# Depthwise causal convolution and token-mixing MLP on one core: the turn of y moves from TensorE to VectorE, the query matmul to 32-row tiles, with new chunks, banks, ring and order

## The chip, the cores and the metric

The kernel runs on one core of a Trainium2 chip. The metric is the device time of one execution in microseconds (us). Three runs of the kernel before took 170.6, 169.86 and 170.9 us; their median is 170.6 us.

## The reference, cut to what matters

```python
w = softmax(weight)                      # 8 heads x 7 taps
y[b, s, h, :] = sum_k w[h, k] * x[b, s - 6 + k, h, :]     # zeros ahead of token 0, 24 channels a head
wq, wk = y @ w_q, y @ w_k                # 192 -> 64
W_tok  = einsum('bsd,btd->bst', wq, wk) / sqrt(64)
mixed  = einsum('bst,btd->bsd', W_tok, y)
out    = relu(mixed) @ w_out             # 192 -> 192
```

`x` is 8 batches x 4224 tokens x 192 channels in float32, 25.95 MB, and `out` has the same size. Both kernels use that the token mix is linear: `mixed = wq @ (w_k^T (y^T y)) / 8`. So for each batch they need the 192x192 matrix `y^T y` (the "gram"), a 64x192 matrix M made from it, and then `relu(wq @ M) @ w_out`, token by token.

## The kernel before, in words

Work goes batch by batch; while batch b is convolved, turned and multiplied, batch b-1 is mixed and stored.

- **Load** (`gen_load`, L483; the DMA is issued at L513 by GpSimd). A batch is cut into 35 chunks of 122 tokens. A chunk lies on 128 partitions: 6 tokens of history and 122 of its own. The DMA turns float32 into bfloat16. `XW` holds all eight batches, so no load waits for a buffer.
- **Convolution** (`gen_conv`, L585). For each pair of heads TensorE multiplies the chunks by a 128x128 band matrix (`BAND`), whole (L315) or as two halves of 64 columns (L316, L317). ScalarE or VectorE moves the result from PSUM to `Y` in bfloat16 (L621): tokens on the partitions, 192 channels in the free dimension.
- **Turn** (`gen_transpose`, L627, and `gen_transpose_hi`, L662). The query matmul needs channels on the partitions. TensorE transposes the first 128 channels of each chunk (L321 whole, or L322 and L323 in halves) and the last 64 channels (L678; two chunks at a time, side by side). VectorE copies these out of PSUM to `YTL` (L648) and `YTH` (L688).
- **Queries** (`gen_wq`, L693). For each of five blocks of tokens TensorE multiplies `w_q` with `YTL` (128 rows, L707) and `YTH` (L711), two column tiles of 64 side by side, 512 tokens in each; a copy brings the result to `WQT` (L728).
- **Gram** (`gen_gram`, L732): three matmuls of 64 columns for each chunk (L744), in a PSUM bank of its own, bank 7. **Mix weights** (`gen_mix_weights`, L758): M from the gram.
- **Mix** (`gen_mix`, L821): M times queries (L836, and L848 or L856), ReLU out of PSUM (L873 on ScalarE, L874 on VectorE), times `w_out` (L902, L920), copy to `OUT` (L941), store from SP (L949).

The order of all this is written out by hand in `PLAN`: a list of turns, each with an operation's number, a letter for its engine or its form on TensorE, and its PSUM bank. Every engine executes its own operations in this order and never passes one that waits. `Program.place` puts in the semaphore waits that the data and the banks ask for.

Of the kernel before, what the change touches and what calls it, by code (L numbers as in the profile page):

```python
# [10 lines left out]
F32 = mybir.dt.float32  # L11


PLAN = """
1D 38G 2D 13G 37G 39G 40G 8D 19D 41G 42G 9D 56G 57G 14D 58G 59G 60G 61G 62G 63G 5D 64G 15P 65G 12D 66G 67G
68G 69G 70G 71G 72G 73G 74G 0S 22D 75G 20D 76G 77G 78G 23D 24D 25A 16P6 6D 79G 80G 21D 11D 81G 26D 27D 17P
4D 28D 18A 29D 30P5 7D 33P6 34D 35D 31A 32A 36P 84F4 85D 90F3 91A 88P1 89D 86P5 87A 116P5 142P 94P2 95D 92F1
93A 96F3 43S 98F6 99A 97D 118F4 117D 106F5 102F1 104F3 82G 100F6 143P 107D 144P 3D 105A 103A 101D 145P 83G
110F5 108F6 109A 112F3 113A 111D 119D 114F0 120F1 115A 126P2 127D 130P6 131D 47A 124F0 48A 125D 46A 44S
122F5 128P2 146P 10D 147P 121D 49A 140P4 53A 50A 132P0 123D 138P3 129D 134P2 141D 148A 149P6 52A 133A 159P4  # L20
157P0 150D 45S 51A 151F6 135A 139D 160A 155F2 158D 161F4 154A 153A 152A 222P6 136P0 162A 137A 211P1 156D
171P4 197P 54A 224A 167P2 168A 213D 165P5 172D 169P0 198P 170A 166D 221P3 210P5 163P0 199P 55A 173F2 223D
225P3 212A 217P5 164A 214P0 226P 174D 179F2 218F 180D 219D 215F 227A 177F2 178D 244F4 175F3 216A 220S 181P5
264P0 233P6 202P 176D 243P2 246A 265A 182D 228P4 232P0 245A 235D 229P 254P6 256A 201P 234A 262P2 230D 231S
185P6 186D 263A 268P4 266P0 267A 200P 255P6 269D 195P3 187P2 196A 203D 239P4 236P0 257D 258P6 240F 188A 241A
183P3 184D 204F2 205A 237F 259F 247P4 250P2 248F 251F 238A 242S 260D 261S 249A 270F0 271A 189P6 190A 304P
276P4 277A 274P0 206P6 252D 253S 272P2 305P 191P4 208A 207A 209A 328P5 275D 273A 317P0 192D 330A 288P2 289D
290P3 278P4 279D 193P5 194D 318F6 329F2 319A 286F0 340F1 280F4 320A 321P5 331A 291D 332P2 287D 342A 335P0
322P 323A 281D 333P 336P 337A 309P 292P4 284F5 334D 338S 324P2 339P0 361P6 363A 325F 293D 282F4 341A 351P6
285D 298P5 353A 326D 327S 373P0 371P2 283D 306P 374A 302P4 303A 294P6 295A 375P0 299D 372D 300P5 301D 369P2  # L30
296P4 297D 362P6 307P 376A 343P0 350P4 370A 346P2 344P 364A 385F6 347F 352A 345D 308P 310D 357P0 348A 349S
365P4 354P2 358P 386D 311F5 312D 355F 356D 359A 360S 387F6 388D 313F5 316A 315A 366F 377F0 383F2 314A 447P5
411P 425P6 378A 384D 379P0 380D 367A 368S 449A 381P3 427A 436P2 438D 412P 424P5 435P0 382A 397P3 395P4 398D
389F2 426A 428P5 396D 431P3 437A 429P 432P 458P0 390D 430A 414P 460A 457P1 459A 442P5 433D 434S 439P3 415P
440F 441A 443F 444D 445S 446P1 468P0 413P 476P3 482P5 470A 448A 399P0 393P1 416P 469P2 483A 417A 477D 400D
478F3 453P5 471A 479A 394D 450P0 418F2 419D 454F 455A 451F 480F3 391F2 409P5 452A 456S 481D 401P6 402A 464P0
461P3 465P 466A 472P6 462P 392D 403P2 410D 463D 467S 492P5 493D 488P0 489A 518P 490P3 404D 407P5 491A 484P0
# [22 lines left out]
913P 924P0 914A 915S 920P2 925P 926A 927S 941F6 943D 921F 932P4 953P0 955D 952P6 933P 922A 923S 940P2 942A  # L60
936P0 954D 937P 956P6 957P 934D 935S 944P2 945F 948P4 949P 938A 939S 958D 959S 946A 947S 950A 951S
""".split()

COL2, ROW2, FULL = "128x64", "64x128", "128x128"


class Op:


    n = 0  # L70
# [134 lines left out]
def bass_lightweight_conv__then__hypermixer_token_mlp_kernel(  # L205
# [11 lines left out]
    GRP = D // H  # L217
# [814 lines left out]
```

## Time and profile before

| | |
|---|---|
| runs | 170.6, 169.86, 170.9 us; median 170.6 us |
| profiled execution | span 168.6 us from the first to the last instruction; the median run is 2.0 us longer than this span |
| instructions in it | 6398 |
| granted TensorE clock, mean | 0.994 |
| DMA packets | 48154, 40.31 MB as written, mean 239 GB/s |
| POOL | 30.3 us busy, nearly all of it issuing the loads |

How to read the lines below: the page's first part gives each engine's busy time and its share of the span. PE is TensorE's matmuls and PEld its weight loads, DVE is VectorE, ACT is ScalarE, POOL is GpSimd, SP the engine that issues the stores. The timeline lists instructions by start in us, then the time to the end of the last one in the row, then the form `out<-in` with partitions x columns, then the count. TensorE's matmuls overlap, so the duration of one (some 0.2 to 0.4 us) is much more than what it costs in a stream: that is read from the distance between starts. The windows view gives busy time by engine in a stretch, the granted clock, the mean busy share of the 16 DMA engines (over 1 where packets overlap) and the bytes written by DMA per second.

### The profile page before, as it was taken

Reading aid. Unit: us, or ns where it says so; the run is one execution under the profiler, and the core shown is the slowest. Engines: PE = TensorE matmul, PEld = TensorE weight load, DVE = VectorE, ACT = ScalarE, POOL = GpSimd, SP = SyncE. Lnnn points to the kernel's source line nnn. Section 1 sums busy time; section 2 is a strip of 40 time slices with the busy share of each in tenths; the row PEclk is TensorE's granted clock in tenths of the full one; section 3 lists DMA queues with packets and bytes.
Section 4 is the critical chain, followed back from the end, with each engine's and each line's share of the span. In section 5 each row is a group of like instructions: output and inputs, shape, how many; then the busy total and the mean of one; then the engine's idle time right before and its main releaser. Section 6 shows DMA issues by size and latency. Waiting matters only on the chain.

```text
span 168.6 us, 6398 instructions
## 1 busy us (share of the span) xinstructions
PE 158.3 (94%) x2874; PEld 116.1 (69%) x2882; DVE 116.2 (69%) x201; ACT 123.8 (73%) x207; POOL 30.3 (18%) x39
## 2 busy tenths in 40 slices
PE   6978999999999999999999999999999999999980
PEld 1458846876677886777865867787778777884640
DVE  5745878774678777566999686875957758578640
ACT  3233699798977869888566978578897889568970
POOL 7999553530503120000000000000000000000000
PEclk9999999999999999999999999999999999999997
DMA  2999999999999999999999999996644463095897
GB/s 23 172 190 185 205 191 196 189 241 301 263 328 208 300 268 276 299 251 317 284 287 199 289 282 341 235 273 232 231 176 190 189 257 149 0 368 218 315 363 283
DMA packets 48154, 40.31 MB, mean 239 GB/s; under 512 B 37632, under 2 KB 40960, under 8 KB 48128
## 3 DMA queue, kind: packets, MB, share of 16 engines
q0 software_dynamic: 36128, 13.61, 67.6%
q1 hardware_dynamic: 12000, 26.31, 43.1%
q8 instruction: 22, 0.36, 0.8%
q14 instruction: 4, 0.03, 0.1%
HBM read 27.56 MB, written 25.95 MB: 317 GB/s over the span
## 4 chain that ended last, share of the span: by engine, by line
PE 78%; ACT 8%; DMA 4%; DVE 3%; issue 2%; POOL 1%; POOLq 0%; ACTq 0%
PE ps L744 14%; PE ps L902 12%; PE ps L920 9%; PE ps L316 8%; PE ps L321 5%; PE ps L836 5%; DMA out_dram<-out_sb 4%; PE ps L678 4%; PE ps L707 4%; ACT y L621 4%; PE ps L711 3%; PE ps L856 3%; PE ps L315 3%; PE ps L322 3%; PE ps L317 2%
## 5 line engine op out<-in xcount | busy, mean ns | idle before, releaser
L621 ACT CAST y<-ps 122x864 bf16<-122x864 f32 (+3 forms) x48 | 37.2, 794 | 11.6 <-PE ps L315 5.8
L873 ACT ACTIVATE rt<-ps 128x1024 bf16<-128x1024 f32 (+3 forms) x56 | 38.7, 725 | 8.3 <-PE ps L836 6.8
L941 ACT COPY out_sb<-ps 128x768 f32<-128x768 f32 (+1 forms) x43 | 32.6, 779 | 11.9 <-PE ps L920 11.3
L513 POOL DMA_DIRECT2D xw<-in_x_dram x34 | 29.9, 909 | 29.4 <-issue 28.6
L941 DVE COPY out_sb<-ps 128x768 f32<-128x768 f32 (+1 forms) x29 | 23.9, 831 | 14.0 <-PE ps L920 12.7
L744 PEld LDWEIGHTS ps<-y 122*64 122x64 bf16 x840 | 29.4, 110 | 5.3 <-issue 2.2
L744 PE MATMUL ps<-y 122*64 122x64 bf16 (+3 forms) x840 | 32.8, 221 | 0.1
L648 DVE COPY ytl<-ps 128x976 bf16<-128x976 bf16 (+1 forms) x40 | 23.3, 592 | 7.2 <-PE ps L321 4.1
L621 DVE CAST y<-ps 122x816 bf16<-122x816 f32 (+3 forms) x24 | 21.5, 902 | 8.1 <-PE ps L317 5.4
L316 PE MATMUL ps<-xw,band 128*64 128x408 bf16 (+2 forms) x104 | 24.9, 342 | 0.0
L317 PE MATMUL ps<-xw,band 128*64 128x408 bf16 (+2 forms) x104 | 24.9, 342 | 0.0
L920 PE MATMUL ps<-wol,rt 64*128 64x192 bf16 (+1 forms) x264 | 23.9, 248 | 0.4
L902 PE MATMUL ps<-woh,rt 64*128 64x192 bf16 x264 | 22.4, 250 | 0.8 <-ACT out_sb L941 0.3
L874 DVE TENSOR_SCALAR rt<-ps 128x512 bf16<-128x512 f32 (+3 forms) x24 | 18.0, 755 | 3.1 <-PE ps L848 1.4
L920 PEld LDWEIGHTS ps<-wol,rt 64*128 64x128 bf16 (+1 forms) x264 | 15.2, 113 | 5.0 <-PE ps L902 2.5
L902 PEld LDWEIGHTS ps<-woh,rt 64*128 64x128 bf16 x264 | 11.7, 114 | 6.8 <-issue 1.8
L728 DVE CAST wqt<-ps 128x512 bf16<-128x512 f32 (+1 forms) x24 | 14.0, 583 | 2.8 <-PE ps L711 2.5
L688 DVE COPY yth<-ps 128x732 bf16<-128x732 bf16 x24 | 12.5, 534 | 4.5 <-PE ps L678 4.2
L902 PE MATMUL ps<-wol,rt 64*128 64x192 bf16 x177 | 15.4, 243 | 0.0
L711 PE MATMUL ps<-yth,wqh 128*64 128x512 bf16 (+1 forms) x72 | 14.9, 361 | 0.0
L707 PE MATMUL ps<-ytl,wql 128*64 128x512 bf16 (+1 forms) x72 | 14.5, 367 | 0.0
L321 PE MATMUL ps<-ident,y 122*128 122x122 bf16 (+1 forms) x159 | 12.0, 217 | 0.9 <-ACT y L621 0.7
(117 smaller groups left out, 209.8 us busy)
## 6 DMA issues: line engine op xcount, KB each, us to landing
out_dram<-out_sb SPq DMA_DIRECT2D x28, 768.0 KB, 7.3
xw<-in_x_dram POOLq DMA_DIRECT2D x7, 816.0 KB, 40.3
xw<-in_x_dram POOLq DMA_DIRECT2D x7, 768.0 KB, 42.9
out_dram<-out_sb SPq DMA_DIRECT2D x8, 384.0 KB, 3.1
xw<-in_x_dram POOLq DMA_DIRECT2D x2, 432.0 KB, 7.3
out_dram<-out_sb SPq DMA_DIRECT2D x8, 96.0 KB, 5.1
xw<-in_x_dram POOLq DMA_DIRECT2D x1, 384.0 KB, 5.1
xw<-in_x_dram POOLq DMA_DIRECT2D x8, 45.8 KB, 28.0
```

The lines of the kernel that those rows point to most:

```text
L316: e.matmul(out[0:64], lhsT[:, 0:64], rhs, **k)
L317: return e.matmul(out[64:128], lhsT[:, 64:128], rhs, **k)
L321: return e.transpose(out, in_, identity)
L513: lambda e, op, part=part: e.dma_start(*part),
L621: return e.copy(dst, src) if op.engine == "ACT" else e.tensor_copy(dst, src)
L648: lambda e, op: e.tensor_copy(YTL[:, t0:t1], bank(mm_l.bank).bitcast(BF16)[:, 0:cols]),
L707: last = e.matmul(ps[64 * i : 64 * i + DH, 0:n], WQL[:, :], YTL[:, starts[i] : starts[i] + n], start=True, stop=False)
L744: mm = e.matmul(bank(GB)[p : p + 64, o : o + z - r], Y[0:w, yb, c, r : r + 64], Y[0:w, yb, c, r:z], start=st, stop=end, skip_group_check=True,
L873: return e.activation(dst, src(), AF.Relu)
L902: last = e.matmul(bank(op.bank + a)[:, (i - q) * D : (i - q) * D + D], RT[p, slot, a if lo else 2, i:n:nt], WOL[p, :] if lo else WOH[p, :] ...
L920: last = e.matmul(bank(fh.bank + a)[:, (i - q) * D : (i - q) * D + D], RT[p, slot, a, i:n:nt], WOL[p, :], start=False, stop=True, skip_gro ...
L941: return e.copy(dst, src) if op.engine == "ACT" else e.tensor_copy(dst, src)
```

## The change

- **Chunks.** A batch is cut into two halves of 2112 tokens, each into 18 chunks of 120 tokens (the last has 72), so 36 chunks in place of 35. A chunk has 8 tokens of history and 120 of its own on 128 partitions. `BAND` now writes 4 blocks of 32 rows, in each 30 tokens and two rows of zeros.
- **Turn.** `gen_transpose` and `gen_transpose_hi` are gone, with their PSUM banks and copies. In `gen_turn` VectorE transposes `Y` to `YT` in blocks of 32x32, from SBUF to SBUF, with two bfloat16 channels taken as one 32-bit word: four instructions a batch, each 128 partitions x 864 words. After it a block of 32 partitions holds 32 pairs of channels of 30 tokens. There is one `YT`, for one batch.
- **Queries.** `gen_wq` makes two passes of nine chunks in each half. A pass is 48 matmuls of 32 rows (one block) x 64 columns of weights x 270 tokens: 3 groups of channel pairs x even and odd x 4 blocks x 2 halves, so eight tiles of the array are addressed in turn, into four PSUM banks. The moving operand takes every second element. Two copies of 128 x 540 a pass put the result in order in `WQT`. `w_q` is loaded with its rows in pairs and four times, once for each block.
- **Banks.** All eight PSUM banks are dealt out by `PLAN`; the gram has none of its own.
- **Ring.** `XW` has six places; loads of batch 6 and 7 wait until the convolutions of batch 0 and 1 have read theirs.
- **Order.** `PLAN` is new throughout, and with it the share of each engine in the copies. Loads aren't issued strictly by batch any more (the second half of batch 3 and the first of batch 4 go ahead of the first half of batch 3). The three scalings of M (`ms`) and the casts of the weights may now go to VectorE too. The first run-up of TensorE's clock is 4 + 4 + 1 whole matmuls.

On TensorE, around the queries of an early batch (at 47.2 us of the trace), this stood before (`ytl`, `yth` are the turned channels, `ident,y` a transposition, `wqt` a mix):

```order
L707 MATMUL ps<-ytl,wql 64x512 x2
L711 MATMUL ps<-yth,wqh 64x512 x2
L848 MATMUL ps<-wqt,mbd 128x512 x2
L321 MATMUL ps<-ident,y 128x122 x2
L321 MATMUL ps<-ident,y 128x76
L848 MATMUL ps<-wqt,mbd 128x512
L321 MATMUL ps<-ident,y 128x122 x8
```

and this stands at the queries of a middle batch now:

```order
L812 MATMUL ps<-woh,rt 128x192 x8
L829 MATMUL ps<-wol,rt 128x192 x8
L625 MATMUL ps<-yt,wq 64x270 x96
L754 MATMUL ps<-wqt,msb 128x512 x4
L762 MATMUL ps<-wqt,mbd 128x512 x2
L276 MATMUL ps<-xw,band 128x432 x6
```

The queries were five groups of four, strewn among transpositions and mixes; now both passes of a batch mostly stand as one block of 96, and no transposition of `y` is left on this engine.

On VectorE this stood before, in a middle batch:

```order
L728 CAST wqt<-ps 128x512
L688 COPY yth<-ps 128x732
L648 COPY ytl<-ps 128x976
L728 CAST wqt<-ps 128x512
L688 COPY yth<-ps 128x732
L648 COPY ytl<-ps 128x320
L648 COPY ytl<-ps 128x976
L941 COPY out_sb<-ps 128x2x384
```

and this now:

```order
L722 TENSOR_SCALAR msb<-ps 128x128
L722 TENSOR_SCALAR mbd<-ps 64x64
L645 CAST wqt<-ps 128x2x9x30
L606 STREAM_TRANSPOSE yt<-y 128x864 x2
L781 TENSOR_SCALAR rt<-ps 128x1024
L606 STREAM_TRANSPOSE yt<-y 128x864 x2
L645 CAST wqt<-ps 128x2x9x30 x2
L592 CAST y<-ps 128x2x18x24
```

The copies of turned channels, 64 in all, are gone; 32 transpositions stand in their place, and more of the ReLUs of 1024 columns (`rt`) do.

The diff, cut to its core:

```diff
-    XW = sbuf("xw", [128, B, NCC, D], BF16)
-    Y = sbuf("y", [128, 2, NCC, D], BF16)
-    YTL = sbuf("ytl", [128, S], BF16)
-    YTH = sbuf("yth", [128, (NCC - SPLIT // CW) * CW], BF16)
+    XW = sbuf("xw", [128, NX, NC, D], BF16)
+    Y = sbuf("y", [128, 2, NC, D], BF16)
+    YT = sbuf("yt", [128, NYT, NC, D], BF16)
...
-    GB = 7
-    planner = Planner(nbank=7)
+    planner = Planner()
...
+        free = [c for (bb, g), ops in conv_of.items() if bb == b - NX for c in ops]
...
+                    needs=[*free, *part[2]],
...
-    def gen_transpose(b, cs):
-                last = turn_halves(e, ps[:, o : o + w], Y[0:w, yb, c, 0:LO], IDENT[0:w, 0:w], op.mode)
...
-                lambda e, op: e.tensor_copy(YTL[:, t0:t1], bank(mm_l.bank).bitcast(BF16)[:, 0:cols]),
...
+    def gen_turn(b, half, k):
+        yb, tb = b % 2, b % NYT
+        c0 = half * NK + k * PASS
+        def turn(e, op):
+            src = Y[:, yb, c0 : c0 + PASS, :].rearrange("p c d -> p (c d)").bitcast(U32)
+            dst = YT[:, tb, c0 : c0 + PASS, :].rearrange("p c d -> p (c d)").bitcast(U32)
+            return e.transpose(dst, src)
+        needs = [*{r.number: r for c in range(c0, c0 + PASS) for r in y_done[b, c]}.values(), *wq_of.get((b - NYT, k), [])]
...
+    def gen_wq(b, k):
+            for j in range(3):
+                for s in range(2):
+                    for i in range(NBLK):
+                        p = slice(32 * i, 32 * i + 32)
+                        for half in range(2):
+                            c0 = half * NK + k * PASS
+                            last = e.matmul(
+                                bank(op.bank[i // 2] + i % 2)[DH * half : DH * half + DH, 0 : PASS * BLK],
+                                WQ6[p, j, s, :],
+                                YT[p, tb, c0 : c0 + PASS, 64 * j + s : 64 * j + 2 * BLK : 2],
+                                start=j == 0 and s == 0,
+                                stop=j == 2 and s == 1,
+                            )
```

More of the change, by code (lines that the diff above doesn't have):

```diff
@@ L11 @@
 F32 = mybir.dt.float32
+U32 = mybir.dt.uint32
 PLAN = """
[L15 to L19, printed above, removed]
```

831 lines of the change are left out of this document (380 added, 451 removed).

## The prediction

> **What bounds the kernel now.** I read the page's first part, its slices and its chain, then the windows, to see which engine has no slack and whether that changes along the run.
>
> ```profile
> PE 158.3 (94%) x2874; PEld 116.1 (69%) x2882; DVE 116.2 (69%) x201; ACT 123.8 (73%) x207; POOL 30.3 (18%) x39
> DVE  5745878774678777566999686875957758578640
> DMA  2999999999999999999999999996644463095897
> GB/s 23 172 190 185 205 191 196 189 241 301 263 328 208 300 268 276 299 251 317 284 287 199 289 282 341 235 273 232 231 176 190 189 257 149 0 368 218 315 363 283
> PE 78%; ACT 8%; DMA 4%; DVE 3%; issue 2%; POOL 1%; POOLq 0%; ACTq 0%
> ```
>
> TensorE is busy 158.3 of 168.6 us and the chain of waits runs through it for 78% of the span, through the DMA for 4%. So TensorE sets the time from the first chunk to the last stores, and what leaves it is worth its whole price until something else has no slack. The windows say what stands next.
>
> ```profile
> 12.00:25.00 13.00, 12.10 (x212) 8.79 (x210) 10.09 (x20) 8.67 (x23) 9.43 (x12) 1.00 1.55 194
> 60.00:80.00 20.00, 19.98 (x362) 14.85 (x361) 13.52 (x22) 16.49 (x27) 0.12 (x1) 1.00 1.32 280
> 140.00:164.00 24.00, 22.85 (x414) 15.32 (x411) 16.72 (x27) 18.85 (x33) 0.00 (x0) 1.00 0.61 228
> ```
>
> (Columns: stretch, then busy us of PE, PEld, DVE, ACT, POOL, the granted clock, the DMA share, GB/s.) From 60 to 80 us TensorE lacks 0.02 us of 20 at the full clock, with ScalarE at 16.5 and VectorE at 13.5. From 140 us, with ScalarE at 79%, it lacks 1.15 us of 24. In the slices the DMA is busy all the time for 27 of 40, up to 114 us, where the loads end: it is off the chain, but has little to give.
>
> **The change part by part.** *Transpositions and old queries leave TensorE.* Their price in a stream is the distance between starts in the timeline; their counts stand in the groups:
>
> ```profile
> 46.13 0.83 PE L678 MATMUL ps<-ident,y 122*64 122x122 bf16 x24
> 46.80 0.22 PE L322 MATMUL ps<-ident,y 122*64 122x122 bf16 x1
> 47.22 0.39 PE L707 MATMUL ps<-ytl,wql 128*64 128x512 bf16 x2
> 47.44 0.38 PE L711 MATMUL ps<-yth,wqh 128*64 128x512 bf16 x2
> 48.56 0.59 PE L321 MATMUL ps<-ident,y 122*128 122x122 bf16 x8
> 49.09 0.36 PE L902 MATMUL ps<-woh,rt 64*128 64x192 bf16 x4
> ```
>
> ```profile
> L321 PE MATMUL ps<-ident,y 122*128 122x122 bf16 x154 | 11.8, 217 | 0.9 <-ACT y L621 0.7 <-issue 0.2
> L678 PE MATMUL ps<-ident,y 122*64 122x122 bf16 x288 | 11.5, 218 | 0.1
> L322 PE MATMUL ps<-ident,y 122*64 122x122 bf16 x118 | 9.1, 217 | 0.9 <-ACT y L621 0.7
> L711 PE MATMUL ps<-yth,wqh 128*64 128x512 bf16 x64 | 13.3, 379 | 0.0
> ```
>
> The high channels: 24 in 46.80 - 46.13 = 0.67 us, 28 ns each, x288 = 8.0 us. The low channels in halves: eight pairs from 46.80 to 47.22, 53 ns a pair, x118 = 6.2 us; whole: eight from 48.56 to 49.09, 66 ns each, x154 = 10.2 us; the eight short chunks 0.4 us. The queries: a pair of 512 columns takes 47.44 - 47.22 = 0.22 us; 64 such pairs (32 of L707, 32 of L711) are 14.1 us, and the eight short blocks some 0.9 us. In all 39.8 us leave TensorE.
>
> *New queries.* 8 batches x 2 passes x 48 = 768 matmuls of 270 columns on tiles of 32 rows. Nothing in this trace has that form, so I bound it. Below: the pair of 512 columns in 0.22 us is 0.43 ns a column, so 270 columns stream in 116 ns; if all eight tiles work at once, that is 14.5 ns a matmul, 11.1 us in all. Above: only the two column tiles work at once, as they do for L707, and the four row blocks take turns: 116 / 2 = 58 ns, 44.5 us. Between them stands how fast one weight load with its matmul can follow another:
>
> ```profile
> 92.79 0.35 PE L316 MATMUL ps<-xw,band 128*64 128x432 bf16 x1
> 92.81 0.35 PE L317 MATMUL ps<-xw,band 128*64 128x432 bf16 x1
> 96.30 0.19 PE L315 MATMUL ps<-gsb,wkt 128*128 128x64 bf16 x1
> 96.38 0.19 PE L315 MATMUL ps<-gsb,wkb 128*128 128x64 bf16 x1
> 55.10 0.66 PE L744 MATMUL ps<-y 122*64 122x192 bf16 x17
> ```
>
> The second half of a convolution starts 20 ns behind the first, with a weight load of its own between them. The matmuls of 64 columns from 96.30 to 96.38 (three steps) stand 27 ns apart, but that is what 64 columns stream in (64 x 0.43 = 28 ns), so they bound the issue only from above. I take 20 ns, the nearest row for neighbours on different tiles: 768 x 20 = 15.4 us. The range keeps 14.5 and 28 ns (11.1 and 21.5 us); 58 ns is a rival.
>
> The page "TensorEngine Tiling (Array Packing)" of the Trainium skill, section "Instruction Overhead", speaks against small matmuls: about 60 cycles each whatever the free dimension, and it warns against splitting a dimension that is already small. At the 2.4 GHz of "TensorE: Matmul & The Clock Gate" that is an estimated 25 ns, 19.2 us in all, 3.8 us more than my term. The 20 ns above is a little under it, so the trace does not fully agree; no run here shows it for 32 rows.
>
> *One chunk more.* 36 in place of 35: the gram's three matmuls, 18 of which (the 17 of the last row and one behind) stand in the half microsecond from 55.10, cost 0.09 us a chunk; the convolution's 8 heads x 24 columns cost 192 x 0.43 = 0.08 us. x8 = 1.4 us.
>
> *TensorE's sum:* 168.6 - 39.8 + 15.4 + 1.4 = 145.6 us of span, if it stays as dense as now.
>
> *VectorE and ScalarE.* The turn replaces copies out of PSUM:
>
> ```profile
> L648 DVE COPY ytl<-ps 128x976 bf16<-128x976 bf16 x32 | 21.0, 661 | 6.7 <-PE ps L321 3.6 <-PE ps L323 3.0
> L688 DVE COPY yth<-ps 128x732 bf16<-128x732 bf16 x24 | 12.5, 534 | 4.5 <-PE ps L678 4.2
> L648 DVE COPY ytl<-ps 128x320 bf16<-128x320 bf16 x8 | 2.5, 316 | 0.5 <-PE ps L321 0.5
> L621 DVE CAST y<-ps 122x864 bf16<-122x864 f32 x8 | 8.3, 1050 | 1.2 <-PE ps L315 0.8 <-PE ps L317 0.4
> L874 DVE TENSOR_SCALAR rt<-ps 128x1024 bf16<-128x1024 f32 x7 | 8.5, 1217 | 0.2 <-PE ps L836 0.2
> L874 DVE TENSOR_SCALAR rt<-ps 128x512 bf16<-128x512 f32 x12 | 8.2, 684 | 2.0 <-PE ps L848 1.4 <-PE ps L856 0.7
> L728 DVE CAST wqt<-ps 128x512 bf16<-128x512 f32 x18 | 12.3, 685 | 1.9 <-PE ps L711 1.8
> ```
>
> Copies of 36.0 us go (21.0 + 12.5 + 2.5). The 32 transpositions of 864 words have no row. Below: at the rate of the 976-column copy, 864 / 976 x 661 = 585 ns. Above: two cycles a word, twice the 864-column cast, 2100 ns. I take that cast itself, 1050 ns, the row with as many 32-bit columns: 33.6 us. Where the order puts the rest: wide ReLUs on VectorE go from 7 to 15 (+9.7 us), narrow ones from 12 to 17 (+3.4), query copies from 24 to 14 (-4), and output copies, convolution copies and the scalings of M together add about 2. VectorE: 116.2 - 36.0 + 33.6 + 9.7 + 3.4 - 4 + 2 = 125 us; ScalarE, which gives the ReLUs away, about 118. On 146 us that is 86% and 81%, where today it is 69% and 73%. No engine but TensorE pays for the turn then, but the cover is thin: in-order engines this full hold PSUM banks longer. The row from 140 us prices it: at 79% TensorE lost 1.15 of 24 us, 4.8%. On the 137 us behind the start that is 6.6 us, of which the present run already has some 1.5. I add 5 us: 150.6, say 151.
>
> The page "Vector Engine (DVE) Microarchitecture Reference", section "The reshape front-end and per-opcode configuration", says that the 32x32 transposition sustains one element per cycle and lane. By it two cycles a word are out and my 1050 ns are about right; no run here shows it yet.
>
> *DMA.* Bytes hardly change, so the DMA gives a floor:
>
> ```profile
> q0 software_dynamic: 36128, 13.61, 67.6%
> q1 hardware_dynamic: 12000, 26.31, 43.1%
> L513 POOL DMA_DIRECT2D xw<-in_x_dram x34: 545/988/1373, 1.3 to 59.6; - x34
> L316 PE MATMUL ps<-xw,band x32: 333/344/370, 109.8 to 138.5; 128*64 128x432 bf16 x16, 128*64 128x408 bf16 x16
> ```
>
> Loads alone (12 to 25 us) run at 194 GB/s as written, stores alone at up to 368 in a slice. The 13.61 MB of loads grow by the rows of history, 8 x 4504 in place of 8 x 4428, to 13.84 MB: 71.3 us; 26.31 MB of stores and weights: 71.5 us. With the first bytes at 2 us this is 145 us, and the last landing makes it 146 of span. The ring adds no wait: batches 6 and 7 need the convolutions of batches 0 and 1, both in the first fifth of the work, while GpSimd was issuing loads until 59.6 us.
>
> *Sum.* 151 us of span; the median run stands 2.0 us over the span of the profile: **153 us**.
>
> **The rivals.**
>
> *Issue-paced queries.* Each matmul on a small tile costs 28 ns, as those of 64 columns and the high transpositions do: 21.5 us, 6.1 more, **159 us**. For it: no row shows four row blocks at work. Against: the 20 ns lead.
>
> *The DMA floor.* All eight tiles work at once (14.5 ns, 141.3 us for TensorE) and the lost 5 us shrink; then the 146 us of transfers end last: **148 us**. For it: 27 full slices. Against: the stores can't run ahead of the mixes.
>
> *Late loads.* By 114 us today the first 27 slices of the GB/s row (6593 in all, x 4.215 us) are 27.8 MB, 14.2 of them stores. A pace 12% faster puts 1.7 MB more of stores into the same time, 4.6 us, and loads end past 120 us. The last convolution starts 30 us before the end today, so it would be wanted at 121, and those of its batch up to 10 us sooner. TensorE then waits about 7 us once: **160 us**.
>
> *VectorE is the bound.* Two cycles a word add 33.6 us: 159 us busy; with some 4 us at each end that its slices leave empty 167, and **169 us** in all, as now.
>
> *Row blocks take turns* (the slower side). If a matmul of 32 rows excludes the other blocks, or its step of two elements halves the stream, a matmul costs 58 ns or more. The point from which the change loses is (39.8 - 1.4) / 768 = 50 ns without any lost time, 43 ns with the 5 us. At 58 ns: 168.6 - 39.8 + 44.5 + 1.4 + 2.0 = 176.7, **177 us** with little lost elsewhere. For it: the step of two elements has no row. Against: column tiles demonstrably overlap with different moving data (L707).
>
> **How the numbers follow.** Forecast 0.43, issue-paced 0.17, DMA floor 0.15, late loads 0.08, VectorE 0.08, row blocks 0.09. Forecast, issue-paced, floor and late loads are faster by over 1%; VectorE splits between faster and the same: faster 0.87, same 0.04, slower 0.09. About 1% is what a measurement of this kernel can tell from no change. The range runs from just under the floor, 147, to 163, which holds the late loads and the issue-paced queries with 3 us over: 0.83 of the chance.
>
> **What would show it.** In the new profile: 768 query matmuls whose 48 take about 1 us from first to last start (0.7 at the floor, 1.3 paced, 2.8 in turns); transpositions of about 1.05 us; VectorE near 125 us and TensorE's share of the span still about 90%; windows in the middle in which TensorE lacks about 1 us of 20; a DMA share over 1 past 114 us. Wrong would be a VectorE that is the chain's main engine, waits of TensorE for `xw`, or a pass of over 2 us.

## The result and the profile after

The changed kernel is slower: 175.34 us (median of 4 runs, 174.33 to 175.64), against 170.32 us for the kernel before (4 runs, 169.86 to 170.9). The ratio is 1.029, with a 95% interval of 1.0243 to 1.0337. The forecast was 153.0 us, 22.3 us less. A median below is of all runs of a kernel; a ratio leaves out disturbed runs (over 1.5% longer, at a lower clock), and where they were several only the ratio is given.

First the page's first part, slices, chain and one line each of the instruction fetch and the stores, of the kernel after:

```profile
PE 145.9 (84%) x2769; PEld 98.3 (57%) x2769; DVE 124.3 (72%) x185; ACT 116.0 (67%) x190; POOL 34.2 (20%) x47
PE   4879398999939799779899996999999999999920
PE 47%; DMA 21%; ACT 10%; DVE 9%; issue 4%; SPq 3%; POOL 1%; ACTq 0%
q8 instruction: 22, 0.36, 0.8%
out_dram<-out_sb SPq DMA_DIRECT2D x28, 768.0 KB, 6.1
```

The work moved as forecast. VectorE is busy 124.3 us (forecast 125), ScalarE 116.0 (118). TensorE fell from 158.3 to 145.9 us. But its slices show nines in a row only in the last third, its share of the span fell from 94% to 84%, and the chain of waits now runs through it for 47% of the time instead of 78%, while the DMA's part went from 4% to 21%. The span is 173.3 us, so TensorE sits idle for 27.4 us where it sat idle for 10.3.

The new operations have rows now (groups by form; timeline):

```profile
L606 DVE STREAM_TRANSPOSE yt<-y 128x864 uint32<-128x864 uint32 x32 | 33.0, 1056 | 1.0 <-PE ps L625 0.7 <-ACT y L592 0.3
```

```profile
130.30 1.81 PE L625 MATMUL ps<-yt,wq 32*64 32x270 bf16 x96
132.04 0.23 PE L282 MATMUL ps<-ident,gsb 128*128 128x128 bf16 x1
```

A transposition takes 1056 ns. Both query passes of a batch, 96 matmuls with as many weight loads, take 132.04 - 130.30 = 1.74 us, 18 ns each. Neither is why the time rose. The windows in 20-us steps, of before and then of after, say where it rose (columns as in the prediction: busy PE, PEld, DVE, ACT, POOL, then clock, DMA share, GB/s):

```profile
0.00:20.00 20.00, 16.78 (x258) 10.85 (x261) 12.37 (x38) 7.72 (x20) 17.99 (x25) 1.00 1.26 153
20.00:40.00 20.00, 19.83 (x352) 14.09 (x347) 14.81 (x24) 17.19 (x31) 7.08 (x8) 1.00 1.54 212
```

```profile
0.00:20.00 20.00, 14.07 (x191) 8.99 (x191) 12.94 (x43) 7.64 (x16) 17.84 (x28) 1.00 1.26 148
20.00:40.00 20.00, 17.31 (x307) 10.88 (x307) 13.36 (x21) 13.63 (x23) 11.56 (x15) 0.74 1.57 194
40.00:60.00 20.00, 15.81 (x395) 11.66 (x394) 11.47 (x17) 11.51 (x21) 4.81 (x5) 0.91 1.41 252
60.00:80.00 20.00, 17.41 (x275) 11.79 (x271) 15.33 (x18) 13.85 (x21) 0.00 (x0) 0.91 1.36 271
100.00:120.00 20.00, 18.33 (x402) 13.49 (x399) 15.27 (x20) 14.61 (x24) 0.00 (x0) 1.00 0.93 223
120.00:140.00 20.00, 19.48 (x425) 13.62 (x421) 16.51 (x25) 16.80 (x27) 0.00 (x0) 1.00 0.63 240
```

Until 80 us TensorE lacks 2.6 to 5.9 us in each window, in three of them at a lower clock, where the kernel before lacked 3.2 us in the first and at most 0.2 in the three behind it; from 120 us on, where the loads are over (share 0.63), it lacks 0.5. So the loss lies where the DMA engines are full. The table of waits and the chain name three places:

```profile
ACT out_sb L847 <- DMA out_dram<-out_sb: 6.7, 3, 3.1
ACT wq L288 <- DMA wq6f<-in_moe_w_q_dram: 3.7, 1, 3.7
PE ps L625 <- ACT wq L288: 3.0, 1, 3.0
PE ps L625 <- issue: 2.5, 2, 1.4
```

```profile
7.71 7.08 DMA xw<-in_x_dram
14.80 0.34 SPq L505
19.95 5.33 DMA whi<-in_moe_w_k_dram
...
42.59 8.12 DMA out_dram<-out_sb
...
64.82 8.72 DMA out_dram<-out_sb
76.16 7.88 DMA out_dram<-out_sb
103.97 1.44 issue
```

SP's first load of weights, before and after, and the two windows behind it, after:

```profile
9.86 0.34 SPq L535 DMA_DIRECT2D wlo<-in_moe_w_q_dram  x1
14.80 1.76 SPq L505 DMA_DIRECT2D wq6f<-in_moe_w_q_dram  x4
20.00:25.00 5.00, 2.98 (x98) 2.18 (x98) 0.90 (x2) 1.59 (x4) 5.00 (x7) 0.57 1.48 203
25.00:30.00 5.00, 4.40 (x32) 1.73 (x34) 3.96 (x9) 3.13 (x7) 2.40 (x5) 0.50 1.59 189
```

- **The start.** SP waits for the load (0,1) before it issues the ten loads of weights. In the new order GpSimd issues that load's last piece late, so SP begins at 14.80 us, for 9.86 in the kernel before, and the last weights land at 25.28. TensorE waits 3.0 us for `w_q`, and the clock granted then is low for 10 us (0.57 and 0.50 in the two windows of 5 us from 20).
- **The output places.** Three times a copy to `OUT` waits for a store to land, 7.9 to 8.7 us after the copy that it waits behind. There are four places, as there were in the kernel before. Behind one of these copies TensorE waits 2.9 us.
- **"Issue".** In the middle of two query passes TensorE waits for nothing that the profile shows. The queue of instructions moves 0.36 MB in 22 packets, 16 KB each.

### The profile page after: what moved, and what is told of

Same layout as the page of the kernel before. It is cut to its first block, busy times and chain, and to the rows that moved or that the text cites. A ratio compares the mean times of both kernels' runs of the same rounds, so it can differ in the third digit from the quotient of the medians.

```text
span 173.3 us, 6163 instructions
## 1 busy us (share of the span) xinstructions
PE 145.9 (84%) x2769; PEld 98.3 (57%) x2769; DVE 124.3 (72%) x185; ACT 116.0 (67%) x190; POOL 34.2 (20%) x47
## 4 chain that ended last, share of the span: by engine, by line
PE 47%; DMA 21%; ACT 10%; DVE 9%; issue 4%; SPq 3%; POOL 1%; ACTq 0%
DMA out_dram<-out_sb 14%; PE ps L660 11%; PE ps L812 8%; PE ps L829 8%; PE ps L625 6%; ACT out_sb L847 5%; DMA xw<-in_x_dram 4%; PE ps L277 4%; PE ps L754 4%; DVE out_sb L847 3%; DMA whi<-in_moe_w_k_dram 3%; SPq L505 3%; ACT rt L780 2%; DVE y L592 2%; PE ps L762 2%
## 5 line engine op out<-in xcount | busy, mean ns | idle before, releaser
L592 ACT CAST y<-ps 128x864 bf16<-128x864 f32 (+1 forms) x48 | 37.1, 806 | 11.2 <-PE ps L278 7.7
L606 DVE STREAM_TRANSPOSE yt<-y 128x864 uint32<-128x864 uint32 x32 | 33.0, 1056 | 1.0 <-PE ps L625 0.7
L660 PEld LDWEIGHTS ps<-y 128*64 128x64 bf16 (+1 forms) x864 | 30.4, 116 | 4.0 <-issue 2.4
L660 PE MATMUL ps<-y 128*64 128x192 bf16 (+4 forms) x864 | 31.9, 228 | 0.4 <-ACT y L592 0.4
L847 DVE COPY out_sb<-ps 128x768 f32<-128x768 f32 x23 | 21.9, 956 | 11.1 <-PE ps L829 10.8
L592 DVE CAST y<-ps 128x864 bf16<-128x864 f32 (+1 forms) x24 | 22.2, 935 | 6.6 <-PE ps L278 3.9
L625 PE MATMUL ps<-yt,wq 32*64 32x270 bf16 x768 | 16.8, 308 | 5.8 <-ACT wq L288 3.0
L277 PE MATMUL ps<-xw,band 128*64 128x432 bf16 (+1 forms) x72 | 17.3, 361 | 1.2 <-ACT wqt L645 0.6
L278 PE MATMUL ps<-xw,band 128*64 128x432 bf16 (+1 forms) x72 | 17.3, 361 | 0.0
L754 PE MATMUL ps<-wqt,msb 64*128 64x512 bf16 (+1 forms) x80 | 14.0, 374 | 3.4 <-ACT out_sb L847 2.9
L625 PEld LDWEIGHTS ps<-yt,wq 32*64 32x64 bf16 x768 | 11.8, 112 | 8.8 <-issue 3.9
L276 PE MATMUL ps<-xw,band 128*128 128x432 bf16 (+1 forms) x72 | 15.2, 351 | 1.7 <-DMA xw<-in_x_dram 1.2
```

The costliest lines, as they stand in the source:

```text
L277: e.matmul(out[0:64], lhsT[:, 0:64], rhs, **k)
L592: return e.copy(dst, src) if op.letter == "A" else e.tensor_copy(dst, src)
L606: return e.transpose(dst, src)
L625: last = e.matmul(bank(op.bank[i // 2] + i % 2)[DH * half : DH * half + DH, 0 : PASS * BLK], WQ6[p, j, s, :], YT[p, tb, c0 : c0 + PASS, 64 ...
L660: mm = e.matmul(at[p : p + 64, o : o + z - r], Y[0:w, yb, c, r : r + 64], Y[0:w, yb, c, r:z], start=st, stop=end, skip_group_check=True,)
L754: last = e.matmul(bank(op.bank[0] + i)[:, 0:n], MSB[p, mb, :], WQT[p, wqb, q0 : q0 + n], start=True, stop=True)
```

## The experiments

All names of lines are the changed kernel's, unless said otherwise. Each kernel stood beside runs of the kernel before on its own chip, whose medians were 170.22 to 170.48 us.

**1. The weights' loads released one load earlier.** The theory: the three waits above add up, the start among them. The rival: VectorE and ScalarE are too full, and TensorE would idle as much without these waits.

```diff
-            "S", emit, needs=load[0, 1], dma=(name, semaphore(f"s_{name}"), 16 * len(pairs)), kind="weights"
+            "S", emit, needs=load[0, 2], dma=(name, semaphore(f"s_{name}"), 16 * len(pairs)), kind="weights"
```

> The changed kernel, but the loads of the weights on SP wait for the first half-batch piece that GpSimd issues second (load[0,2]) and not for the one it issues last (load[0,1]). Theory start: w_q arrives some 6 to 8 us sooner than the 21.5 us of the changed kernel, the 3 us wait of TensorE for its cast, the 5 us wait of VectorE for w_out's cast and the half clock from 20 to 30 us are gone; 168 us (166 to 171). Theory ring (the four places for outputs are what costs): the gain is given back at the first waits for a place, near 50 us; 172 to 175. Rival bandwidth (the DMA as a whole is too slow for the new order, wherever it waits): no gain, 174 to 176.

171.47 us (171.37 to 171.82), ratio to the kernel before 1.007 [1.0044, 1.0096]: 3.9 us less than the changed kernel. In the window from 20 to 40 us the clock is 1.00 again:

```profile
20.00:40.00 20.00, 18.29 (x384) 12.16 (x380) 16.01 (x24) 15.95 (x26) 11.52 (x15) 1.00 1.58 198
```

The mean clock is 0.98 for 0.934, so a part of the 3.9 us is waiting and a part is the clock.

**2. Six output places for four.**

```diff
-    NX, NYT, NRT, NOUT = 6, 1, 3, 4
+    NX, NYT, NRT, NOUT = 6, 1, 3, 6
```

> The changed kernel with six places for outputs in SBUF in place of four. Theory ring: ScalarE's 6.7 us of waits for stores are gone, with TensorE's 2.9 and 2.0 us behind them and the lower clock from 50 to 55 and 75 to 80 us; 168 us (166 to 171). Theory start: the stretch to 35 us is as before and the rest gains little; 173 to 175. Rival bandwidth: no gain, the waits move elsewhere; 174 to 176.

171.02 us (169.76 to 173.92), ratio 1.0033 [1.0004, 1.0062]: 4.3 us less than the changed kernel. The wait of ScalarE for `out_dram` fell from 6.7 to 1.2 us (VectorE waits 0.6).

**3. Both.**

> Both edits. Start and ring together: the gains add up, 161 us (158 to 165), with TensorE lacking less than 1.5 us in each 20 us from 30 to 140 us. If only one of them is a cause: as that one alone, about 168. Rival bandwidth: 172 or more, with a DMA share over 1 to the end of the loads and TensorE waiting for x.

167.5 us (167.29 to 169.5), ratio 0.986 [0.9798, 0.9923]: 7.8 us less than the changed kernel, close to 3.9 + 4.3. It beats the kernel before, but by far less than was expected of it, so the two waits are not the whole cause. What was left in this kernel:

```profile
PE ps L625 <- issue: 5.9, 3, 3.0
PE ps L276 <- DMA xw<-in_x_dram: 1.5, 1, 1.5
ACT out_sb L847 <- DMA out_dram<-out_sb: 1.2, 1, 1.2
```

```profile
48.30 1.60 PE L625 MATMUL ps<-yt,wq 32*64 32x270 bf16 x76
52.85 0.89 PE L625 MATMUL ps<-yt,wq 32*64 32x270 bf16 x20 [2.95 <-issue]
```

After 76 of 96 query matmuls TensorE stands still for 2.95 us. The granted clock then costs about as much again (windows of 3 us of the same kernel):

```profile
50.00:53.00 3.00, 0.15 (x8) 0.15 (x16) 0.07 (x1) 0.00 (x0) 0.00 (x0) 0.80 1.61 194
53.00:56.00 3.00, 3.00 (x42) 1.47 (x35) 1.78 (x2) 1.49 (x3) 0.00 (x0) 0.50 1.60 191
56.00:59.00 3.00, 3.00 (x28) 1.96 (x24) 1.64 (x4) 1.25 (x3) 2.86 (x3) 0.56 1.60 192
```

TensorE is busy all the time from 53 to 59 us and gets 0.50 and 0.56 of its clock: another 2.8 us (3 x 0.50 + 3 x 0.44). The two shorter stalls of the same kernel, 1.35 us at 20 us and 1.63 us at 96 us, cost no clock: it is 1.00 in the windows of 3 us behind them.

**4. The same delay in the kernel before.** Is the start a price of the new order, or did the old kernel merely not have it? The weights' loads of the kernel before wait for one load more.

```diff
-        return add("SP", emit, 1700, needs=load[0, 1], dma=(name, semaphore(f"s_{name}"), 16 * 3), tail=4000, vt=vt)
+        return add("SP", emit, 1700, needs=load[0, 3], dma=(name, semaphore(f"s_{name}"), 16 * 3), tail=4000, vt=vt)
```

> The kernel before, with the loads of the weights waiting for the fourth piece of batch 0 and not the second, so that they are issued about 5 us later, as in the changed kernel. Theory start: it costs the old kernel too, 173 to 176 us, with TensorE idle and its clock lower between 20 and 30 us. Rival (the old order has slack there, so the start is no cause by itself): 170 to 171.

174.13 us (172.85 to 176.03), ratio 1.0199 [1.0142, 1.0256], by which it is 3.4 us more, with 17.06 us of TensorE from 20 to 40 us at a clock of 0.91 (19.83 at 1.00 before). SP begins with the weights at 14.67 us here, as late as in the changed kernel. A late start costs either kernel some 3.5 to 4 us: the kernel with the old turn and the old queries pays it too, so it is a price of where the semaphore stands in the order of the loads.

**5. No later loads of x**, on the kernel of experiment 3. All work of the compute engines stays, with an eighth of the loading of x; every convolution reads batch 0 and waits for its loads alone.

```diff
+            if b:
+                part = (
+                    XD[0:1, b, len(load[b, gi]) + 4 * gi, :],
+                    bass.AP(x_t, (base + len(load[b, gi]) + 4 * gi) * D, [[D, 1], [1, 16]]),
+                    part[2],
+                )
...
-                        XW[:, s, c0 : c0 + n, GRP * h : GRP * h + GRP],
+                        XW[:, 0, c0 : c0 + n, GRP * h : GRP * h + GRP],
```

> The changed kernel with the weights' loads released by load (0,2) and six output places, in which only batch 0 of x is loaded: batches 1 to 7 convolve batch 0's tokens again, and their loads are replaced by copies of 32 bytes. It leaves out seven eighths of the loading of x; all work of the engines stays. With the loads the same kernel took 167.5 us, with 5.9 us of TensorE and 6.8 us of its weight loads behind issue in the query passes and stores that landed 7.5 us late. Theory (the load traffic crowds out stores and the fetch of TensorE's instructions): the waits for issue at the query passes and for out_dram vanish, stores land in under 5 us, and the time falls to 151 to 156 us, where the prediction's sum stood. Rival (VectorE and ScalarE, 124 and 116 us busy, hold TensorE up by themselves): the time stays above 162 us, and the idle time of TensorE is put down to ScalarE and VectorE.

159.55 us (158.92 to 159.97), ratio 0.9353 [0.9307, 0.9399]: 8.0 us less than with the loads, between the two expectations. The page and the groups of this kernel (its lines are 7 higher):

```profile
PE 139.5 (89%) x2769; PEld 95.2 (60%) x2769; DVE 123.5 (79%) x185; ACT 115.8 (74%) x190; POOL 22.8 (14%) x47
L632 PE MATMUL ps<-yt,wq 32*64 32x270 bf16 x768 | 15.3, 290 | 0.9 <-DVE yt L613 0.5 <-DVE out_sb L854 0.2
out_dram<-out_sb SPq DMA_DIRECT2D x28, 768.0 KB, 4.4
```

No wait of the query matmuls for issue is left (0.9 us on their weight loads), no wait for `out_dram`, and a store lands in 4.4 us in place of 7.5. So the load traffic is what made both. GpSimd issues less here too (22.8 us busy for 34.1), but with the loads its last issue is at 59.1 us, and a stall of 1.63 us still comes at 96.30 us. The run also shows what the change is worth undisturbed, 6.5 us over the forecast; the next section says of what.

**6. The changed kernel as it is, without the later loads** (four places, weights behind load (0,1); the edit of experiment 5 on it).

> The changed kernel as it is (four output places, weights' loads behind load (0,1)), in which only batch 0 of x is loaded; it leaves out seven eighths of the loading of x. Theory (four places are too few only because stores land 8 us late beside the loads): the waits of 6.7 us for out_dram vanish without a fifth place; what is left over the 159.55 us of the kernel with both repairs and no later loads is the start, 3 to 4 us: 162 to 164 us. Rival (four places are too few by themselves, with stores of 4 us): the waits for out_dram stay at 3 us or more, and the time is 165 to 168 us.

163.57 us (162.21 to 164.16), ratio 0.9576 [0.9525, 0.9626]: 11.8 us less than the changed kernel. The wait for `out_dram` is gone with four places. Four are too few only because the stores land late beside the loads. What is left over experiment 5 is 4.0 us; the two kernels differ in the start and in the places, and no wait for a place is left, so that is the start again.

**7. The kernel before, without the later loads** (the same edit on it).

> The kernel before the change, in which only batch 0 of x is loaded: batches 1 to 7 convolve batch 0's tokens again, and their loads are copies of 32 bytes. It leaves out seven eighths of the loading of x. Theory (the old kernel, whose TensorE was busy for 94%, had its transfers behind it, and the load traffic became a cost only with the change, which gains 8 us without the later loads): 168 to 170.5 us, at most 2 us less than with them. Rival (load traffic costs both kernels alike, by the fetch of instructions and by late stores, and is no part of why the change lost): 161 to 164 us.

169.58 us (169.24 to 169.59), ratio 0.9935 [0.991, 0.996]: 0.7 us less. The old kernel had its transfers behind TensorE's work, and the traffic cost it next to nothing; it costs the changed kernel 11.8 us. Without the later loads the changed kernel, as it is, is the faster of the two, 163.57 us for 169.58. Of everything tried this says most about the sign.

**8. Three places in the x ring for six**, the loads given out as places come free, on the kernel of experiment 3.

```diff
-    NX, NYT, NRT, NOUT = 6, 1, 3, 6
+    NX, NYT, NRT, NOUT = 3, 1, 3, 6
...
+            held.append(turn) if turn.endswith("G") else turns.append(turn)
...
+            for load in list(held):
+                first = int(load[:-1])
+                if all(x.number in seen for x in self.ops[first].needs + self.ops[first].after):
...
+                    turns.append(load)
```

> The same kernel as in the run of both repairs (167.5 us) with three places in the x ring in place of six; a load of x is given out only once the convolutions that read its place are over. All work is the same. Theory (loads far ahead crowd out stores and instruction fetch in the first 110 us): the loads spread over 140 us, the share of the DMA engines in 30 to 110 us falls, waits for issue fall from 6 us to under 3, and the time is 160 to 165 us. Rival (the loads need all the time they can get, as the ring of six was meant to give): waits of TensorE for xw come in behind 60 us, and the time is 169 to 175 us.

167.83 us (167.26 to 168.59), ratio 0.9845 [0.9796, 0.9893], as with six. The premise failed: GpSimd gave its last load out at 91.0 us in place of 59.1, but the DMA engines were as full as before (a share of 1.24 and 1.59 in the windows of 10 us from 40 to 60 us and 1.44 from 100 to 110, for 1.28, 1.60 and 1.43 with six). A load still took up to 43.3 us from issue to landing (60.1 with six), so most likely the loads queue for longer than the ring holds them back. The waits for issue of the query passes were 6.4 us. It sets nothing apart.

**9. Two places**, so that they would be held back further.

> The run of both repairs (167.5 us) with two places in the x ring: a load is given out only once the convolutions two batches back are over, so that the loads come in eight bursts of some 9 us with pauses between. All bytes are still moved. Without the later loads the same kernel took 159.55 us; with three places the loads did not spread (DMA share 1.2 to 1.6 up to 110 us as with six) and the time was 167.8. Theory (what costs 8 us is that the DMA engines are full without a pause until 110 us, so that a store and a packet of instructions wait behind queued loads): the waits for issue in the query passes fall from 5.9 to under 3 us, there are windows with a DMA share under 0.8 ahead of 100 us, and the time is 161 to 165 us. Rival (the bytes themselves cost it, whenever they are moved, or the loads are now late): the waits for issue stay at 5 to 6 us or waits of TensorE for xw of more than 3 us take their place, and the time is 167 us or more.

Ratio 1.0013 [0.9974, 1.0052], some 170.7 us: 3 us slower than with six. In the profiled execution, of 172.58 us, the waits for issue of the query passes were 4.8 us, and 3.9 us more stood at other matmuls; TensorE waited 3.1 us for `xw`. The expected pauses hardly came: the share was 0.94 and 1.02 in the windows from 60 to 80 us and above 1.1 up to 130. This goes to the rival as far as the time is concerned; a kernel that moves all the bytes with real pauses was not found.

**10. Two x places and four output places.**

> The kernel of two x places with four output places in place of six. Theory (four places suffice once the stores no longer stand behind queued loads): within 1.5 us of the kernel with two x places and six output places, and waits for out_dram of under 3 us in all. Rival (the stores still land 7 us late inside the bursts): 3 to 4 us more, with waits of 5 us or more for out_dram.

173.98 us (171.46 to 175.69), ratio 1.0236 [1.018, 1.0292]: the rival again. The waits for `out_dram` come back, 5.2 us on ScalarE and 2.8 on VectorE, with stores of 7.9 to 8.4 us in the chain.

**11. The query passes set apart.** 192 instructions in 1.74 us might outrun the fetch of instructions.

```diff
-... 107C 100W40 112A ... 250C 262A 251C 239D 282C5 252A 240W06 284A 238D 243W24 ...
+... 100W40 107C 112A ... 240W06 250C 262A 251C 239D 282C5 252A 284A 238D 243W24 ...
```

> The same kernel as in the run of both repairs (167.5 us), with the two query passes of batches 0, 2, 3 and 4 set apart: one to three matmul groups of the Gram matrix or of the output stage that stood ahead of both now stand between them. Nothing is added. Theory (192 instructions in 1.6 us outrun the fetch of TensorE's instructions): the wait for issue in the query passes falls from 5.9 us to under 3.5 us and the time by 1 to 3 us, to 164.5 to 166.5. Rival (the fetch is held up by loads wherever it falls, since the number of instructions is the same): the waits for issue move to other lines, and the time stays within 1 us of 167.5.

Ratio 0.9965 [0.9919, 1.0011], some 169.8 us: 2 us slower than the kernel it was made from. The waits at the query passes fell from 5.9 to 2.1 us, and new ones came at the gram (profiled execution, of 170.99 us):

```profile
PEld ps L660 <- issue: 4.5, 10, 1.7
PE ps L660 <- issue: 2.2, 2, 1.7
PE ps L625 <- issue: 2.1, 1, 2.1
```

The gram too has a weight load to each matmul, of 64 to 192 columns. The stall moved on, as the rival said; where to is counted behind experiment 12. In time neither came true.

**12. Half of the query matmuls left out**, so that a pass has half the instructions.

```diff
-                for s in range(2):
+                for s in range(1):
...
-                                stop=j == 2 and s == 1,
+                                stop=j == 2,
```

> The run of both repairs (167.5 us), in which each query pass multiplies only the even channels: 24 matmuls with 24 weight loads in place of 48 and 48, so half of the query products are left out; all else, the loads of x too, stays. The 384 matmuls that go are worth 384 x 18 ns = 6.9 us by the pace of the passes. Theory (two passes in a row, 192 instructions in 1.74 us, outrun the fetch of instructions while the loads run): the waits for issue at the query passes, 5.9 us in all, fall under 2 us as well, and the time falls by 10 to 13 us, to 155 to 158. Rival (the waits for issue come wherever a packet of instructions is due beside full queues, dense or not): they stay at 4 us or more, at this or other lines, and the time falls by 7 us at most, to 160.5 or more.

Ratio 0.9527 [0.949, 0.9564], 162.3 us by the two shorter of its four runs (162.21 to 167.04 us in all); the kernel with all of them stood at 167.87 on the same chip. By these two the time fell by 5.6 us, less than the 6.9 us of the work left out, but the waits for issue at the passes did fall as the theory had it:

```profile
q8 instruction: 19, 0.31, 0.7%
PE ps L276 <- DMA xw<-in_x_dram: 4.5, 3, 2.3
PE ps L625 <- issue: 1.8, 2, 1.1
```

So each theory was half right. Shorter passes stall less (1.8 us for 5.9 or 6.0). What that gained was taken by the next limit, waits for `xw` of 4.5 us: at this pace the loads themselves come late.

*Where the stalls stand.* Counting TensorE's matmuls and weight loads from the start of each trace ties the stalls to the packets of instructions. The table gives how long the weight loads waited for issue behind that many instructions (all such waits over 1 us):

| instructions ahead | both repairs (3) | changed kernel | passes apart (11) | half the queries (12) | no later loads (5) |
|---|---|---|---|---|---|
| 442 or 443 | 1.65 us | none | 1.69 us, at the gram | 1.30 us | none |
| 1456 | none | none | none | 1.06 us | none |
| 1711 or 1712 | 3.26 us | 1.38 us | 2.45 us | none | none |
| 3233 | 1.93 us | 1.76 us | none | none | none |

From 443 to 1712 it is 5 x 253.8 instructions, from 1712 to 3233 6 x 253.5, and from 442 to 1456 4 x 253.5; 2769 matmuls and as many weight loads, shared out over 22 packets, are 252 each. So the stalls stand whole packets apart, whichever line the order puts there, and experiment 11 only put the gram at the first place. Not every boundary between packets has one, but those behind the densest stretches: in the kernel of both repairs, while the loads run, the 254 instructions ahead of the three stalls took 4.2, 3.1 and 3.2 us, ahead of the other boundaries 5.0 to 11.8 us, with no wait over 0.6 us there. Behind the loads, at 142.7 us, 254 took 3.7 us and no stall followed. In the kernel before no such stretch took under 5.3 us. In the changed kernel TensorE had waited 3.0 us for `w_q` shortly ahead of the first of these boundaries.

**13. Both repairs once more**, on the chip of experiment 12.

> The run of both repairs once more, in the call of the one with half the query products, so that the two stand beside the same runs of the kernel before: 167.5 us again, a ratio to the kernel before of 0.984 to 0.988, if the first measurement holds; a ratio of over 0.992 would say that the repairs together gained less than the 7.8 us that the first one showed.

167.87 us (166.59 to 168.87), ratio 0.9834 [0.9797, 0.9872]. No kernel that computes all of the reference was found to be faster, and the one with three places (167.83 us) is as fast.

**14. The first piece of the other half first**, since the first convolution waited for its load until 10.2 us (7.8 before the change).

```diff
-50G 28D 23D 29D 30D 25C0 ... 39C1 51G 42C2 ... 80F3 84F4 82F5 ...
+47G 28D 23D 29D 30D 25C0 ... 39C1 51G 42C2 ... 64F3 68F4 66F5 ...
```

> The same kernel as in the run of both repairs (167.5 us), with one thing moved: GpSimd gives out the loads of the first piece of the first half first, and TensorE convolves that piece first, before the piece of the other half. Theory (the first convolution starts when its load lands, 10.2 us instead of 7.8 us before the change): the first convolution starts 1.5 to 2.5 us earlier and the time falls by as much, to 165 to 166 us. Rival (the start is bound by the weights of the query step, which stand behind the same loads): the first convolution starts earlier, TensorE then waits as long for wq, and the time stays at 167 to 168 us.

168.66 us (167.94 to 169.65), ratio 0.9898 [0.9865, 0.993]: no gain. From 0 to 10 us TensorE is busy 6.89 us for 5.63, from 10 to 20 only 6.98 for 9.05: it then waits 3.0 us for the next piece of `xw`. The wait moved, but to the load, not to `wq` as the rival had it.

**15. The last short block of 64 tokens ahead of the last large ones**, because 6.6 us lie between the last copy and the end (3.9 before the change).

```diff
+... 801D 839R6 840C5 842A 827R2 830A 841D 798S 843R5 844F ... 845A 808F 802S 846S ...
-... 839R2 813D 840C4 842A 834S 841A 843R5 814S 844F 845A 846S
```

> The run of both repairs (167.5 us) with the last block of 64 tokens of the last batch computed and stored some twenty operations earlier (with a place of its own for its ReLU output); in the changed kernel it is the last work of all. Before the change 3.9 us lay between the end of the last output copy (164.67) and the end of the span; after it 6.6 us, because two small stores are given out one after the other behind the eight large ones. Theory (the order puts a short block last, and its stores end the program): the distance falls from 6.6 to about 4 us, and the time by 2 to 3 us, to 164.5 to 165.5. Rival (the large stores end last anyway, the queue is full): the distance stays, and the time is within 1 us of 167.5.

169.03 us (167.86 to 169.31), ratio 0.9894 [0.9852, 0.9936]. The distance stayed: the last copy ended at 160.9 us and the span at 167.5. The large stores end last anyway: SP gives the last of them out at 163 us.

**16. The same with eight output places.**

> The run of the last block moved ahead, with eight output places in place of six. Theory (one wait of 1.2 us for a store is left with six): 0.5 to 1.5 us less than with six, 164 us if the last block gives what is expected, and no wait of ScalarE or VectorE for out_dram. Rival (that wait is covered by the waits for issue next to it): the same time within 0.5 us as with six.

169.64 us (168.46 to 170.64), ratio 0.9963 [0.9932, 0.9995]. The last wait for `out_dram` is gone, and it bought nothing: the rival.

## Why the prediction was wrong

Point by point, by its own steps.

- **What TensorE bounds.** Right for the kernel before, and experiment 7 shows it more sharply than the chain did: without seven eighths of the loads it gains 0.7 us.
- **What leaves TensorE and the new queries.** Right. The queries' term was 15.4 us; the group's busy time without load traffic is 15.3, and a block of 96 takes 18 ns a matmul where 20 was taken, between the bounds of 14.5 and 28. That 20 came so near is in part luck: it was the lead of one pair, and other pairs of halves in the same trace start 0 to 50 ns apart (L322 and L323 both at 46.80 us, L316 and L317 at 93.84 and 93.89). The issue-paced queries (28 ns) and the row blocks that take turns (58 ns) are out. So is the estimate of 25 ns that the prediction drew from the page "TensorEngine Tiling (Array Packing)" of the Trainium skill, section "Instruction Overhead": by it 96 would take an estimated 2.4 us, and they took 1.74.
- **VectorE and ScalarE.** Right in size: 1056 ns for 1050, 124.3 us for 125, 116.0 for 118. VectorE as the bound is out. The page "Vector Engine (DVE) Microarchitecture Reference" of the Trainium skill, section "The reshape front-end and per-opcode configuration", gives one element per cycle and lane; the row agrees with it, as 864 words took as long as the cast of 864 columns (1050 ns) and not twice that.
- **The step that failed: "145.6 us of span, if it stays as dense as now", and the 5 us added for lost density.** The forecast held the idle time at 10.3 + 5 = 15.3 us. It was 27.4. And it held TensorE's busy time at 158.3 - 39.8 + 15.4 + 1.4 = 135.3 us; it was 145.9, 142.7 with both repairs and 139.5 without the later loads. Most of that goes with the clock, for which the forecast had no term: by the windows, the three below 1.00 are worth an estimated 7.5 us at most (17.3 x 0.26 + 15.8 x 0.09 + 17.4 x 0.09), and the one of both repairs 2.8 (16.6 x 0.17). The price of lost density was read from a window after the loads had ended (from 140 us), where the cover is thin but transfers are quick. Two thirds of the program run beside full queues, and no row was looked up for what a late store, late weights or a late packet of instructions cost there.
- **"The DMA gives a floor".** This step treated the transfers as bytes, and asked only whether they end in time. They do. But what a transfer costs the chain is how late one lands: the three stores waited for took some 8 us. The old kernel waited 0.2 us for `out_dram`, with four places too and stores no quicker (a median of 7.3 us in its page, 6.1 in the changed kernel's, 7.5 with both repairs). That a shorter step of TensorE asks for a place sooner is argued from this; no run sets the step alone.
- **"The ring adds no wait"** held: no convolution of batch 6 or 7 waited for its load's place.
- **The new order.** The step counted what each engine does in it, and not in which order GpSimd issues the loads that SP waits for. That the weights would go out later (14.80 us for 9.86) could be read from that order.

The sums by the runs: 175.34 - 11.8 (the later loads, experiment 6) - 4.0 (the start, experiments 5 and 6) = 159.5. From there to 153.0 are 6.5 us, 6.7 as spans (157.3 for 150.6). TensorE's busy time has 4.2 of them (139.5 for 135.3), at a full clock, which no single row explains. The idle time has 2.5 (157.3 - 139.5 = 17.8 for 15.3). Against the 10.3 us of the kernel before it has grown by 1.9 ahead of 20 us (5.1 for 3.2; the first load of x is waited for until 10.0 us), by 3.5 between, and by 2.1 at the end. So for the middle the 5 us were enough once the loads are away; the two ends had no term. What the loads cost was followed by repairs only in part: six places bring 4.3 us with the start as it is; 8.0 us stay.

Of the rivals on record none was the cause. Waits for `xw` were 1.2 us, not 7; they do appear as soon as TensorE is made faster still (experiment 12). Of the three things that the prediction said would show it wrong, VectorE as the chain's main engine (it has 9%) did not come about, and a pass of over 2 us only with a stall inside it: the second of the two passes from 102.58 us took an estimated 2.5 us (103.45 to 105.9), an undisturbed one 0.87.

**Shown:** the delayed weights, the four output places, and that both the late stores and the stalls called issue hang on the load traffic. **Shown for the place of the stalls, not for the time that they cost:** that they stand at the boundaries of packets of instructions behind dense stretches. That the packet itself waits behind queued loads is argued from this and from experiment 5; no view gives the landing of one packet. **Open:** whether the 8.0 us that stay could be had back with all bytes moved. No schedule of loads that leaves pauses was found, and a version with larger packets was not tried.

## What to carry to other kernels

When work leaves the bounding engine, add to the sum of its terms what its waits will cost at the new pace, from rows of the stage with the fullest queues, not of the quietest: how late a store lands against how soon its buffer is wanted again. Follow each semaphore on which a load is held back through a new order, weights above all, before anything is costed. And try the kernel without the traffic, old and new: 0.7 us against 11.8 told more than any row. Where an engine waits for nothing that the profile shows, count the instructions ahead of each such wait, in more than one order: equal counts at different lines point to the fetch.

## What the runs showed of the hardware that was not expected

- Eight tiles of 32 rows x 64 columns, with a weight load for each matmul, run at 18 ns a matmul over 96 of them, near the 14.5 ns that eight tiles sharing 116 ns of streaming would give.
- Beside full DMA engines (a share of 1.6) TensorE stood up to 3.0 us in the middle of a run of short matmuls with nothing to wait for but issue. These stalls stand behind the same number of TensorE's instructions in different orders (443, 1712, 3233), where 254 instructions had run in 3.1 to 4.2 us; without the later loads none is left there, though 254 took as little.
- After a gap of about 3 us TensorE ran for some 6 us at a granted clock of 0.50 to 0.56, although it was busy throughout: a wait of 3 us costs nearly 6. Gaps of 1.35 and 1.63 us in the same kernel cost no clock.
